# Gated unit on one core: second product's low part earlier in the ring, second half's weights on another queue, last rows' pieces respread

## The chip, the cores and the metric

The kernel runs on one core of one Trainium2 chip. The metric is the device time of one execution in microseconds (us); the median of the runs is what is compared. One execution was also profiled, and its trace gives the start and the length of each instruction on each engine: TensorE (PE, with its weight loads as PEld), VectorE (DVE), ScalarE (ACT), GpSimd (POOL), and SyncE (SP), which here only issues DMAs. Each engine works through its own instructions in order; semaphores make one wait for another.

## The reference

One block of a transformer in float32, for 2048 rows of 576 columns:

```
mod = (silu(c) @ w_mod) as six rows sa, ca, ga, sb, cb, gb of 576
h = layernorm(x) * (1 + ca) + sa
x = x + ga * (attention(h; 32 heads of 18, softmax over all 2048 keys) @ wo)
h = layernorm(x) * (1 + cb) + sb
x = x + gb * ((sigmoid(h @ w_gate) * (h @ w_up)) @ w_down)
```

The gated unit is the last line: w_gate and w_up are 576 x 4608, w_down is 4608 x 576.

## The kernel before, in words

Every product is formed from high and low parts: an operand is rounded to a shorter format for TensorE (the high part, F32R) and what the rounding dropped is a second operand (the low part). A product is high x high + high x low + low x high. "Low" stands below for making such a low part, a subtraction.

Attention comes first and takes the time up to about 1597 us of the trace. Near its end, the rows of its second half (rows 1024 to 2047) still lack the last 192 of 576 columns of the output projection; those columns go to DRAM (`oend`), the partial sums too (`x1p`), and the gated unit finishes these rows beside its own work.

**The gated unit** (from line 986 on) runs over two halves of the rows (1024 rows each), over 18 blocks of 256 of the 4608 columns, and over seven products in each block: gate and up together are formed in a scheme of seven products for a 2 x 2 split (in place of eight), so that some operands are sums of weight parts. `ORDER = (1, 6, 2, 7, 5, 4, 3)` is the order of the products. The loop at L1236 runs over `seq`, all 252 pairs of block and product; this document calls one pass a **turn**, numbers the turns of a block 0 to 6, and calls the turn number overall n. So turn 0 is product 1, turn 1 product 6 (the "second product"), turn 2 product 2, turn 3 product 7, turn 4 product 5, turn 5 product 4, turn 6 product 3.

In a turn TensorE does `product` (L1050): 14 matmuls, seven for the gate half and seven for the up half, which use the weight's high part (a = 0, 1, 2) and low part (a = 3, 4). The first low operand is the third matmul of each half. At turns 1 and 3 it also does `down` (L1090), the second matrix product of the block before: eight accumulators of six matmuls each, out of a pool of three PSUM banks, and VectorE adds each to the output (`Oa`, L1094). After a product VectorE adds up partial sums in PSUM (L1253 at turn 1, L1264 at turn 3, L1269 at turn 4, L1275 at turn 5, L1280 at turn 6). At turns 2, 4, 5 and 6 a quarter of the gated values is finished (`gate`): sigmoid on ScalarE (L1059, L1062), multiplication on VectorE (L1060, L1063), rounding on ScalarE (L1065), and the low part on VectorE (`gate_low`, L1070).

**The weights** come through a ring of five tiles (`wgp`, LOOK + 1 buffers). In the first half, three steps make the weights of a product:

- `weights_sums` (L998), on POOL: S1, S2, S3, the sums of raw weight parts that products 5, 6 and 7 use, made at turn 3 for the next block; at turn 1 S2 is rewritten for product 3, once product 6's low has read it. Emitted for turn n + 5, at the end of turn n.
- `weights_high` (L1018), on ScalarE (L1031): the rounding, for turn n + 4.
- `weights_low` (L1034), on VectorE: two subtractions, L1040 on 128 partitions and L1041 on 64, and then a DMA on SP (L1042) that stores the finished tile (640 KB) into `ws` in DRAM. `LOWS` says at which turn which low is made: an entry d at turn t makes that of turn t + d. The first one of a turn stands ahead of `gate_low`, the others behind it and behind a piece of the last rows.

In the second half, the same tiles are read back from `ws` (L1025), at the beginning of the turn four ahead, into the ring slot that the turn before has given up. Each block's w_down (`wd`, 1152 KB) is loaded by SP (L1074) at turn 4, into a single buffer that the down product of turn 3 has just given up.

**Order.** From turn n = 7 (`ORDERED`) the order on PE, DVE and ACT is that of the program text (`manual_schedule`); before it, and on POOL and SP throughout, the scheduler of the framework places instructions. A wait in one of these engines' instructions holds all that stands behind it there.

**The last rows** (`last_rows`, L1131) are a generator: each call of `next` does one piece, and its `yield` tells the loop what follows. Its pieces, in order: for two groups of four row tiles, a load of the columns (`od`), an empty one, a transposition with rounding into `oh` and `ol`, another with rounding into `om` (L1159 to L1161), and four projections (L1177, L1180); then for two groups, loads, an empty one, two statistics pieces (L159), a power on POOL, two Newton steps (L176 to L179), two normalisations, an empty one, and six transpositions that ScalarE modulates (L1185) and a DMA stores to `hs`; and last, three times, a load of tiles `B`, an empty one, and seven operand pieces: a subtraction on POOL (L740), a rounding on ScalarE (L729), a low part on POOL (L731, L736), and a store to `xs` on SP. The operands in `xs` are loaded for the second half in the last block of the first (L1305).

In the loop, a piece is done at turns 1 and 3 of each block, at every turn while `light` is true, and a second one at turn 1 unless the first yielded true:

```python
if n >= ROWS_FROM and (at in (1, 3) or light):
    light = next(rows2, None)
while lows:
    weights_low(n + lows.pop(0))
if n >= ROWS_FROM and at == 1 and not light:
    light = next(rows2, None)
```

The functions that the diff touches, and what calls them:

Of the kernel before, what the change touches and what calls it, by code (L numbers as in the profile page):

```python
# [15 lines left out]
F32 = mybir.dt.float32  # L16
# [25 lines left out]
DL = 384  # L42
ORDER = (1, 6, 2, 7, 5, 4, 3)
LOOK = 4
LOWS = ((1, 2), (2,), (2,), (2, 3, 4), (), (), ())
NB = F // 256
LAG = 2

# [2 lines left out]
SIDES = ((0, 0), (0, 1), (1, 0), (1, 1))  # L51
TURNED = ((0, 1), (0, 0), (1, 1), (1, 0)), ((0, 1), (1, 1), (0, 0), (1, 0))
ORDERED = 7
ROWS_FROM = 7
SECOND = 7 * NB


# [1 line left out]
def tile_block(ctx, tc, x_in, wqkv, wo, w_gate, w_up, w_down, c_in, w_mod, out):  # L59
    nc = tc.nc  # L60
# [105 lines left out]
    def ln_scales_steps(pool, mv, rs):  # L166

        n = rs.shape[-1]
        var = pool.tile([P, n], F32, name="var")
        sd = pool.tile([P, n], F32, name="sd")  # L170
        r0 = pool.tile([P, n], F32, name="r0")
        nc.vector.tensor_scalar_add(var, mv[:, :, 1], EPS)
        nc.gpsimd.tensor_tensor(r0, var, powers[:, 0:n], op=ALU.pow)
        yield True
        for to in (r0, rs):
            nc.vector.tensor_mul(sd, r0, r0)  # L176
            nc.vector.tensor_mul(sd, sd, var)
            nc.vector.tensor_scalar(sd, sd, -0.5, 1.5, op0=ALU.mult, op1=ALU.add)
            nc.vector.tensor_mul(to, r0, sd)  # L179
            yield to is r0  # L180

    def ln_apply(z, xt, mean, rs):

# [322 lines left out]
    with tc.tile_pool(name="wv1", bufs=1) as wvp:  # L506
        tiles = [[(o + D * w, P)] for o in (128, 256, 384) for w in (0, 1)] + [[(DM, 64), (D + DM, 64)]]
        for i, parts in enumerate(tiles):
# [5 lines left out]
            for g in range(2):  # L514
                pl = project_qk([(wt, 2 * g), (wt, 2 * g + 1)], run if i else None)
                col, n = parts[-1]
# [189 lines left out]
    def ln_spill(zs, ch, psum, pool, put):  # L706


        for g in range(2):
            for i in range(3):  # L710
                pt = psum()
                for j, z in enumerate(zs):
                    nc.tensor.transpose(pt[:, j * P : (j + 1) * P], z[:, g, i * P : (i + 1) * P], ident)
                ev = pool.tile([P, 512], F32, name="ev", bufs=2)
                c = 3 * g + i
                put(ev, pt, mcol2[:, 0, c : c + 1], mcol2[:, 1, c : c + 1])
                nc.sync.dma_start(hs[g, i, :, ch * 512 : (ch + 1) * 512], ev)
                yield c < 5

    def operand_parts(half, i, blocks, parts, hi, lo_eng, queue):  # L720

# [170 lines left out]
    for u in range(UNITS):  # L892
# [6 lines left out]
        for kt in range(NT):  # L899
# [6 lines left out]
            for does in (("vtmmttmvtm", "tmttkwmtmm") if plain else ("vmmttmmtvt", "mtkttmwmmt"))[kt % 2]:  # L906
# [16 lines left out]
                else:  # L923
                    c, h = next(sides)
# [93 lines left out]
    def weights_high(st, k):  # L1018

        w = wgp.tile([P, 2, 5, P], F32R, name="w")  # L1020
        st["w", k] = w
        kept = ws[st["b"], ORDER.index(k)]
        flat = w.rearrange("p v a c -> p (v a c)").bitcast(F32)
        if st["half"] == 1:
            nc.scalar.dma_start(flat, kept.bitcast(F32))  # L1025
            return
        A11, A12, A21, A22 = parts_of(st)
        src = {1: A11, 2: A12, 4: A22}.get(k)
        if src is None:
            src = st[{5: "S1", 6: "S2", 7: "S3", 3: "S2"}[k]]  # L1030
        nc.scalar.copy(w[:, :, 0:3, :], src)  # L1031
        st["src", k] = src
# [87 lines left out]
    for n in range(LOOK):  # L1120
        weights_sums(n)
        weights_high(block(n), seq[n][2])
    weights_low(0)
    weights_sums(LOOK)
    load(1, 0)
    load_x(4, "k2")
# [4 lines left out]
    def last_rows():  # L1131


        def psum():
            return pd.tile([P, 512], F32, name="d")

        with tc.tile_pool(name="fin", bufs=1, side="right") as pool:
            w = pool.tile([P, 2, 2, D], F32R, name="w")
            nc.gpsimd.dma_start(w, wod)
            for t0 in (0, 4):  # L1140
                od = pool.tile([P, 4, 256], F32, name="od")
                nc.sync.dma_start(od[:, :, 0:192], oend[:, t0 : t0 + 4, :])
                nc.sync.dma_start(od[:, :, 192:256], oend[:, t0 : t0 + 4, 128:192])
                yield True
                yield
                pt = psum()
                for j in range(4):
                    nc.tensor.transpose(pt[:, j * P : (j + 1) * P], od[:, j, 0:P], ident)
                oh = pool.tile([P, 512], F32R, name="oh")
                ol = pool.tile([P, 512], F32R, name="ol")  # L1150
                nc.vector.tensor_copy(oh, pt)
                nc.vector.tensor_sub(ol, pt, oh.bitcast(F32))
                yield
                pt = psum()
                for j in range(4):
                    nc.tensor.transpose(pt[:, j * P : (j + 1) * P], od[:, j, P:256], ident)
                om = pool.tile([P, 512], F32R, name="om")
                omh = pool.tile([P, 512], F32R, name="omh")
                nc.vector.tensor_copy(om[0:64], pt[0:64])  # L1159
                nc.vector.tensor_copy(omh[64:P], pt[64:P])  # L1160
                nc.vector.tensor_sub(om[64:P], pt[64:P], omh[64:P].bitcast(F32))  # L1161
                xts = []
                for j in range(-1, 4):
                    if j < 3:
                        xts.append(pool.tile([P, D], F32, name="xt", bufs=2))
                        nc.sync.dma_start(xts[-1], x1p[:, t0 + j + 1, :])
                    if j < 0:
                        yield
                        continue
                    rows = slice(j * P, (j + 1) * P)  # L1170
                    xt = xts[j]
                    for h in range(2):
                        cols = slice(h * HALF, (h + 1) * HALF)
                        acc = psum()
                        ts_ = ((oh, 0, 0), (oh, 1, 0), (ol, 0, 0), (om, 0, 1), (om, 1, 1))
                        for n, (a, i, k) in enumerate(ts_):
                            nc.tensor.matmul(  # L1177
                                acc[:, :HALF], a[:, rows], w[:, i, k, cols], start=n == 0, stop=n == 4
                            )
                        nc.vector.tensor_add(xt[:, cols], xt[:, cols], acc[:, :HALF])  # L1180
                    nc.sync.dma_start(x1d[:, t0 + j, :], xt)
                    yield

        def modulated(ev, pt, scale, bias):
            nc.scalar.activation(ev, pt, AF.Identity, scale=scale, bias=bias)  # L1185

        with tc.tile_pool(name="zp2", bufs=1, side="right") as zp:
            for ch in (2, 3):
                zs = []
                for t in range(4 * ch, 4 * ch + 4):  # L1190
                    z = zp.tile([P, 2, 384], F32, name="z", bufs=4)
                    for g in range(2):
                        nc.sync.dma_start(z[:, g, 0:HALF], x1d[:, t - 8, g * HALF : (g + 1) * HALF])
                    zs.append(z)
                yield True
                yield
                for j, z in enumerate(zs):
                    ln_stats(zp, z[:, :, 0:HALF], mv2[:, 4 * ch + j, :])
                    if j % 2:
                        yield  # L1200
                four = slice(4 * ch, 4 * ch + 4)
                yield from ln_scales_steps(zp, mv2[:, four, :], rs2[:, four])
                for j, z in enumerate(zs):
                    ln_rows(z, 4 * ch + j, z[:, :, 0:HALF], nc.vector)
                    if j % 2:
                        yield j > 1
                yield True
                yield from ln_spill(zs, ch, psum, zp, modulated)
        with tc.tile_pool(name="xop2", bufs=2) as pool:

            def get():
                return [pool.tile([P, 512], F32, name="B", bufs=5) for _ in range(5)]

            def parts():
                return pool.tile([P, 2, 512], F32R, name="ho", bufs=3)

            for i in range(3):
                blocks = get()
                for (g, r), t in zip(((0, 0), (0, 1), (1, 0), (1, 1)), blocks):
                    cols = slice(HW + r * 512, HW + (r + 1) * 512)  # L1220
                    nc.sync.dma_start(t, hs[g, i, :, cols])
                yield True
                yield True
                for _ in operand_parts(1, i, blocks, parts, nc.scalar.copy, nc.gpsimd, nc.sync):
                    yield True
# [5 lines left out]
        return t[:, 512 * v : 512 * (v + 1)]  # L1231

    rows2 = last_rows()
    light = False
    before = None
    for n, (hf, b, k) in enumerate(seq):  # L1236
        if n == ORDERED:
            manual.enter_context(tc.manual_schedule(engines={mybir.EngineType.PE, mybir.EngineType.DVE, mybir.EngineType.Activation}))
        st, kept = block(n), None
# [14 lines left out]
        elif k == 2:  # L1254
# [4 lines left out]
            kept = gate(st, None, 0, 0)  # L1259
# [5 lines left out]
        elif k == 5:  # L1265
# [4 lines left out]
            kept = gate(st, st["u3"], 1, 1)  # L1270
            down_weights(st)
        elif k == 4:
# [3 lines left out]
            kept = gate(st, st["p1"], 1, 0)  # L1276
        else:
# [3 lines left out]
            kept = gate(st, st["u2"], 0, 1)  # L1281
# [4 lines left out]
        at = n % 7  # L1286
        lows = list(LOWS[at])
        if lows:
# [3 lines left out]
        if n >= ROWS_FROM and (at in (1, 3) or light):  # L1292
            light = next(rows2, None)
        while lows:
            weights_low(n + lows.pop(0))
        if n >= ROWS_FROM and at == 1 and not light:
            light = next(rows2, None)
        weights_sums(n + LOOK + 1)
        if at in (0, 4):
# [36 lines left out]
```

## Time and profile before

| what | value |
|---|---|
| median of three runs | 2979.63 us (2979.29 to 2982.65) |
| the profiled execution's own time | 2975.26 us |
| its span, first to last instruction | 2973.5 us |
| PE busy | 2863.7 us, 96% of the span |
| DVE busy | 2208.8 us, 74% |
| ACT busy | 1564.3 us, 53% |
| POOL busy | 709.2 us, 24% |
| mean granted TensorE clock | 0.987 |
| `ws` stores on SP, loads of `w` on ACT | 126 and 126, 640 KB each |

The profile lists, for each group of instructions, the line of the kernel, the engine, the operation, "output <- input" by the program's names, the shapes, and how many. In a timeline, a row gives the start, the length, the instruction, and in brackets how long the engine had been idle before it and who released it. A list of waits gives, for each pair, the total, the number of times, and the longest. A stretch ("windows") gives the busy time of each engine between two points, the granted clock (1.00 is full), the share of the DMA engines' time, and GB/s. The chain is the work that ended last, followed back from the end. Because matmuls are pipelined, a row of many matmuls is a little longer than the distance to the next.

### The profile page before, as it was taken

How to read it: one execution, taken by the hardware profiler on the slowest of the kernel's cores; microseconds unless marked ns; L12 is line 12 of the kernel's file. 1: busy time of each engine (PE TensorE's matmuls, PEld its weight loads, DVE VectorE, ACT ScalarE, POOL GpSimd, SP SyncE). 2: the span in 40 equal slices, each digit the busy share in tenths (PEclk: the TensorE clock that was granted, in tenths of full speed). 3: DMA queues.
4: the chain of work that ended last, by engine and by line, in shares of the span. 5: the costliest groups of instructions: out<-in, count | busy, mean ns of one | idle time of the engine just before them, and what ended most of it. 6: DMA issues, size and time to landing. Idle time of an engine off the chain costs nothing.

```text
span 2973.5 us, 46334 instructions
## 1 busy us (share of the span) xinstructions
PE 2863.7 (96%) x17141; PEld 1892.2 (64%) x17141; DVE 2208.8 (74%) x4015; ACT 1564.3 (53%) x2941; POOL 709.2 (24%) x869
## 2 busy tenths in 40 slices
PE   7999999999999999999999999899989999999998
PEld 6964333333344444444445888788877888888887
DVE  7277888888899989999874777778777555555555
ACT  3216889999987779988786222233333111111111
POOL 3122024445122112750112222222463100000000
PEclk9999999999999999999999999999999999999999
DMA  5344124333212111321236556565776844555443
GB/s 170 122 160 124 57 69 139 138 130 123 75 57 63 47 38 50 107 84 47 79 108 232 192 192 219 183 233 191 271 243 238 313 157 171 166 170 173 159 157 125
DMA packets 136386, 429.26 MB, mean 144 GB/s; under 512 B 19100, under 2 KB 55968, under 8 KB 123872
## 3 DMA queue, kind: packets, MB, share of 16 engines
q1 hardware_dynamic: 101520, 261.62, 25.9%
q10 hardware_dynamic: 18144, 82.58, 8.4%
q0 software_dynamic: 16496, 82.10, 7.9%
q8 instruction: 135, 2.21, 0.3%
q14 instruction: 91, 0.75, 0.1%
HBM read 267.77 MB, written 157.95 MB: 143 GB/s over the span
## 4 chain that ended last, share of the span: by engine, by line
PE 80%; DVE 9%; ACT 5%; DMA 2%; issue 2%; POOL 1%; SPq 1%; ACTq 0%; DVEq 0%; POOLq 0%
PE x L1050 18%; PE o L551 16%; PE d L1090 15%; PE s L449 11%; PE s L927 10%; PE s L277 3%; ACT p L931 3%; PE s L688 2%; PE s L328 2%; DVE w L1040 1%; DVE w L1041 1%; DVE mx L455 1%; DMA ws<-w 1%; DVE hl L1070 1%; ACT hh L1065 1%
## 5 line engine op out<-in xcount | busy, mean ns | idle before, releaser
L455 DVE TENSOR_REDUCE mx<-s 128x1 f32<-128x512 f32 x1696 | 1076.1, 683 | 122.5 <-PE s L449 107.7
L931 ACT ACTIVATE p<-s 128x512 f32<-128x512 f32 x2048 | 1068.7, 610 | 147.8 <-PE s L449 78.0
L449 PE MATMUL s<-k,q 54*128 54x512 f32 x1920 | 607.7, 450 | 13.0 <-ACT p L931 5.9
L551 PE MATMUL o<-p,vaug 128*32 128x512 f32 x4096 | 554.1, 606 | 0.4 <-ACT p L931 0.4
L927 PE MATMUL s<-q,k 56*128 56x512 f32 x1920 | 551.7, 425 | 0.7 <-DMA q<-mrows 0.2
L1090 PE MATMUL d<-wd,hh 128*128 128x288 f32 x2304 | 462.8, 295 | 11.9 <-DVE Oa L1094 11.9
L927 PEld LDWEIGHTS s<-q,k 56*128 56x128 f32 x1920 | 260.2, 186 | 293.4 <-DVE mx L455 183.8
L449 PEld LDWEIGHTS s<-k,q 54*128 54x128 f32 x1920 | 273.2, 184 | 250.4 <-ACT p L931 170.4
L1050 PE MATMUL x<-k,w 128*128 128x512 f32 x1512 | 379.1, 405 | 43.4 <-DVE w L1040 40.5
L1094 DVE TENSOR_TENSOR Oa<-Oa,d 128x288 f32<-128x288 f32 x576 | 260.2, 454 | 173.5 <-PE d L1090 169.6
L1090 PEld LDWEIGHTS d<-wd,hh 128*128 128x128 f32 x2304 | 375.4, 189 | 19.6 <-DVE Oa L1094 13.6
L1050 PEld LDWEIGHTS x<-k,w 128*128 128x128 f32 x1512 | 292.7, 196 | 110.8 <-DVE w L1040 47.3
L1090 PE MATMUL d<-wd,hl 128*128 128x288 f32 x1152 | 341.0, 296 | 0.0
L1062 ACT ACTIVATE u<-u 128x512 f32<-128x512 f32 x72 | 45.5, 632 | 421.6 <-DVE u L1269 381.1
L1050 PE MATMUL x<-big,w 128*128 128x512 f32 x1008 | 236.8, 390 | 2.6 <-DVE u L1269 2.6
L1050 PE MATMUL x<-w,w 128*128 128x512 f32 x1008 | 235.8, 391 | 0.0
L1090 PEld LDWEIGHTS d<-wd,hl 128*128 128x128 f32 x1152 | 217.0, 188 | 0.0
L1050 PEld LDWEIGHTS x<-big,w 128*128 128x128 f32 x1008 | 188.3, 188 | 44.0 <-issue 4.4
L1050 PEld LDWEIGHTS x<-w,w 128*128 128x128 f32 x1008 | 187.9, 188 | 37.3
L1059 ACT ACTIVATE sg<-x 128x512 f32<-128x512 f32 x36 | 21.5, 599 | 346.9 <-PE x L1050 346.7
L551 PEld LDWEIGHTS o<-p,vaug 128*32 128x32 f32 x4096 | 83.4, 108 | 164.0 <-issue 152.3
L1096 POOL DMA_DIRECT2D out_dram<-Oa x16 | 8.7, 544 | 620.8 <-DVE Oa L1094 620.7
(215 smaller groups left out, 3002.4 us busy)
## 6 DMA issues: line engine op xcount, KB each, us to landing
ws<-w SPq DMA_DIRECT2D x126, 640.0 KB
w<-ws ACTq DMA_DIRECT2D x126, 640.0 KB
wd<-wds SPq DMA_DIRECT2D x36, 1152.0 KB
k<-kd SPq DMA_DIRECT2D x60, 360.0 KB
wds<-w POOLq DMA_DIRECT2D x18, 1152.0 KB, 4.5
k<-kd SPq DMA_DIRECT2D x60, 180.0 KB
w<-in_B_w_down_dram POOLq DMA_DIRECT2D x18, 576.0 KB, 4.6
q<-qd SPq DMA_DIRECT2D x64, 144.0 KB
```

Source lines behind the costliest of these rows:

```text
L277: nc.tensor.matmul(acc, w, hT[:, t, cols], start=n == 0, stop=n == len(ts_) - 1)
L328: nc.tensor.matmul(acc[:, 0:HALF], hT[:, k, rows], w, start=n == 0, stop=n == len(ts_) - 1,)
L449: nc.tensor.matmul(sp, qs[rows, qt * P : (qt + 1) * P], ks[rows, at * 512 : (at + 1) * 512], start=True, stop=True,)
L455: nc.vector.tensor_reduce(to, sp, axis=AX.X, op=ALU.max)
L551: nc.tensor.matmul(acc[32 * j : 32 * j + 32, :], vaug[:, kt, (2 * p + h) * VW : (2 * p + h) * VW + 32], probs[2 * c + h], start=kt == 0, s ...
L688: nc.tensor.matmul(acc[:, :HALF], a, w, start=i == 0, stop=i == len(ts_) - 1)
L927: nc.tensor.matmul(sT, ks[rows, kcols], qs[rows, c * 512 : (c + 1) * 512], start=True, stop=True)
L931: state["exp"] = nc.scalar.activation(pr, sT, AF.Exp, scale=SCALE)
L1050: nc.tensor.matmul(acc[v], w[:, v, a, :], X[s][:, b, :], start=first and n == 0, stop=n == 6, skip_group_check=not first,)
L1062: nc.scalar.activation(t[:, 0:512], t[:, 0:512], AF.Sigmoid)
L1090: nc.tensor.matmul(acc[:, :HALF], a[:, f, rows], w[:, f, cols], start=n == 0, stop=n == 5)
L1094: nc.vector.tensor_add(Oa[:, t, cols], Oa[:, t, cols], acc[:, :HALF])
```

## The change

- `LOWS`: the low of product 6 leaves turn 0, where it was made one turn ahead of its use, for turn 5 of the block before, three turns ahead (`(3,)` at index 5). There it stands ahead of that turn's `gate_low`. Since block 0 has no block before it, the loop is preceded by the lows of turns 0 and 1 in place of turn 0 alone.
- The second half's reads of `ws` (L1025) are issued by SP in place of ACT.
- The last rows start at n = 4 in place of 7, and `light` now has three values: True (a further piece at once, and at turns 1 and 3 a second one behind it), None (a second one at turn 1 alone), and 0 (neither). The piece that makes `om` yields 0, so that no projection follows in its turn. An empty piece behind a load now falls into the same turn as the load; of the operand pieces and of the modulated transpositions, two are done at turn 3.

Worked out from the two loops, in n (block:turn): the first rounding `oh`, `ol` moves from 10 (1:3) to 8 (1:1), the first `om` from 15 (2:1, with a projection in the same turn) to 8 (1:1), the first projection from 15 to 10 (1:3); the second `oh`, `ol` from 29 (4:1) to 24 (3:3). Statistics, Newton steps and normalisations keep their turns. Operand pieces were at 87 to 111, with a load and an empty piece between the three groups, seven of them in block 15; they are now at 86 to 105, one of them in block 15.

```diff
-LOWS = ((1, 2), (2,), (2,), (2, 3, 4), (), (), ())
+LOWS = ((2,), (2,), (2,), (2, 3, 4), (), (3,), ())
...
-ROWS_FROM = 7
+ROWS_FROM = 4
...
             nc.vector.tensor_mul(to, r0, sd)
-            yield to is r0
+            yield True if to is r0 else None
...
                 nc.sync.dma_start(hs[g, i, :, ch * 512 : (ch + 1) * 512], ev)
-                yield c < 5
+                yield True if c < 5 else None
...
         if st["half"] == 1:
-            nc.scalar.dma_start(flat, kept.bitcast(F32))
+            nc.sync.dma_start(flat, kept.bitcast(F32))
             return
...
-    weights_low(0)
+    for n in range(2):
+        weights_low(n)
...
                     if j < 0:
-                        yield
+                        yield 0
                         continue
...
                     if j % 2:
-                        yield j > 1
+                        yield True if j > 1 else None
...
     rows2 = last_rows()
-    light = False
+    light = True
...
-        if n >= ROWS_FROM and at == 1 and not light:
+        if n >= ROWS_FROM and (at == 1 and light is None or at in (1, 3) and light is True):
             light = next(rows2, None)
```

## The prediction

> **What bounds the kernel now.** I read the page first, then the stretches of the gated unit, then what TensorE waits for in each. A turn is one of the seven products of a block, turns 0 to 6 in ring order; "low" is the pair of VectorE subtractions L1040 and L1041.
>
> ```profile
> span 2973.5 us, 46334 instructions
> PE 2863.7 (96%) x17141; PEld 1892.2 (64%) x17141; DVE 2208.8 (74%) x4015; ACT 1564.3 (53%) x2941; POOL 709.2 (24%) x869
> ```
>
> ```profile
> 1598.00:2347.00 749.00, 690.67 (x3692) 602.61 (x3693) 549.78 (x947) 221.57 (x342) 236.53 (x207) 0.96 0.65 232
> 2347.00:2973.00 626.00, 617.03 (x3438) 549.61 (x3436) 342.79 (x607) 106.60 (x176) 7.61 (x14) 1.00 0.49 164
> ```
>
> TensorE is busy 96% of the span, so only what it waits for can be won. The two stretches are the gated unit's first half (18 blocks, and 4 turns of the next) and the rest of the second; columns are length, busy PE, PEld, DVE, ACT, POOL, granted clock, DMA share and GB/s. The second is full: 617 of 626 us, clock 1.00. The first has 58 us of idle PE and a clock of 0.96. TensorE's waits from 1599 to 2347 us (total, times, longest), then those of the second half:
>
> ```profile
> PE x L1050 <- DVE w L1040: 40.5, 14, 4.3
> PE d L1090 <- DVE Oa L1094: 10.5, 6, 6.0
> PE d L1177 <- DVE om L1161: 2.9, 1, 2.9
> PE x L1050 <- DVE u L1269: 2.6, 5, 1.0
> ...
> PE x L1050 <- DVE w L1041: 0.4, 1, 0.4
> ```
>
> ```profile
> PE d L1090 <- DVE Oa L1094: 1.4, 1, 1.4
> ```
>
> The first row is the target: nearly once a block TensorE waits for a low. Block 4 shows which, first on PE, then on DVE:
>
> ```profile
> 1740.03 3.35 PE L1050 MATMUL x<-k,w 128*128 128x512 f32 x14
> 1743.21 6.51 PE L1050 MATMUL x<-big,w 128*128 128x512 f32 x28
> 1749.56 3.79 PE L1050 MATMUL x<-k,w 128*128 128x512 f32 x16
> 1755.72 3.01 PE L1050 MATMUL x<-k,w 128*128 128x512 f32 x12 [2.38 <-DVE w L1040]
> ```
>
> ```profile
> 1744.81 1.29 DVE L1269 TENSOR_TENSOR u<-x,u 128x512 f32<-128x512 f32 x2
> ...
> 1748.24 1.28 DVE L1275 TENSOR_TENSOR p<-x,p 128x512 f32<-128x512 f32 x2
> ...
> 1751.01 0.69 DVE L1070 TENSOR_TENSOR hl<-p,hh 128x512 fp32r<-128x512 f32 x1 [0.69 <-ACT hh L1065]
> 1751.62 1.28 DVE L1280 TENSOR_TENSOR u<-x,u 128x512 f32<-128x512 f32 x2
> ...
> 1754.38 0.69 DVE L1070 TENSOR_TENSOR hl<-u,hh 128x512 fp32r<-128x512 f32 x1 [0.68 <-ACT hh L1065]
> 1754.99 0.68 DVE L1040 TENSOR_TENSOR w<-S,w 128x512 fp32r<-128x512 f32 x1
> 1755.70 0.42 DVE L1041 TENSOR_TENSOR w<-S,w 64x256 fp32r<-64x256 f32 x1
> 1756.16 0.69 DVE L1040 TENSOR_TENSOR w<-raw,w 128x512 fp32r<-128x512 f32 x1
> 1756.88 1.13 DVE L1041 TENSOR_TENSOR w<-raw,w 64x256 fp32r<-64x256 f32 x1
> 1758.04 1.50 DVE L1253 TENSOR_TENSOR u<-x,p 128x512 f32<-128x512 f32 x2
> 1759.56 0.46 DVE L1094 TENSOR_TENSOR Oa<-Oa,d 128x288 f32<-128x288 f32 x1
> 1760.36 0.45 DVE L1094 TENSOR_TENSOR Oa<-Oa,d 128x288 f32<-128x288 f32 x1 [0.34 <-PE d L1090]
> ```
>
> Turns 4, 5, 6 and 0 have no down product; each costs TensorE 3.18 us (two issue in 6.35, 1743.21 to 1749.56). VectorE needs 3.4 us for each of turns 4 to 6 (1748.24 to 1751.62): two adds, the multiplication, 0.69 idle for ScalarE's rounding, the low part of h. It starts late, and only then comes the low of product 6. TensorE does product 1 and two matmuls of product 6 (x16), then stops.
>
> **Part 1, the low of product 6 at turn 5.** It now stands in front of L1070 in turn 5, into the 0.69 us hole ahead of 1751.01; its 0.68 + 0.42 us are done near 1751.5, 1.8 us before x16 ends. So the wait goes: 40.5 + 0.4 = **40.9 us**. What ScalarE must round first is there: the low already follows turn 4's rounding, in its old place too. The low's store goes along on SP, among the loads of the next block's weights; its slot in the ring is not wanted again before turn 2, so this costs nothing, and were it late, ScalarE's rounding would wait there. With the wait goes a slower clock behind it; the first and the last of the 15 resumptions, by the chain (block 4's above took 3.01):
>
> ```profile
> 1668.61 4.57 PE x L1050 x12
> ...
> 2280.99 4.47 PE x L1050 x12
> ```
>
> Six of the 15 take 3.0; the excess of the other nine over that, 1.4 to 2.8 each, adds up to **15.8 us**.
>
> [...] The gap of 3.02 us before 1668.61 was followed by a slow stretch, so here I go by the rows.
>
> **What is late next.** The 1.12 us do not vanish; they fill the hole and push turn 6 by 0.4. Then the second low of turn 0 and L1253 follow, and L1253 stands ahead of the down products' sums in VectorE's order. Without the wait, block 4's down product would start at 1755.91 (1749.56 + 6.35); with three accumulators of 0.8 us each (the spacing of the L1094), the fourth waits for the first L1094 at 1758.3. VectorE then ends L1253 at 1759.54 - 1.17 + 0.43 = 1758.8, L1094 at 1759.3: a wait of **up to 1.0** us. POOL's rewriting of S2 moves with the low: it slowed turn 0's second L1041 (1.13 against 0.42), giving 0.7 back there, and now falls beside turns 5 and 6. Ends 0.2 and 1.0; I take 0.6 for each of the 11 blocks that are not in the operand pieces: **+6.6**.
>
> Some blocks carry a piece of the last rows at turn 3, in front of the lows. Rows: a statistics piece, one operation of a Newton piece, and what statistics did at turn 6:
>
> ```profile
> L159 DVE BATCH_NORM_STATS2 st<-z x16: 406/442/461, 1861.6 to 2011.2; 128x6 f32<-128x288 f32 x16
> ```
>
> ```profile
> 1904.88 0.16 DVE L179 TENSOR_TENSOR rs<-r,sd 128x4 f32<-128x4 f32 x1
> ```
>
> ```profile
> 1867.37 3.44 PE L1050 MATMUL x<-big,w 128*128 128x512 f32 x14 [0.96 <-DVE u L1269]
> ```
>
> Four of the former are 1.8 us, 0.96 of which TensorE waits already; with the two aggregations 1.0 more will show, twice. The Newton piece has four of the latter: 0.65, twice. The rounding of the attention's columns (two operations on a 128x512 tile, each like L1040's 0.69) is now at block 3, with the transposes on TensorE as some relief: 1.0. **+4.3**.
>
> **Part 3, the pieces spread.** They start at turn 4 of block 0 and no longer idle two turns at a time. At block 2 the rounding into `om` and a projection shared a turn: 2.9 us and, as behind most such gaps, some 1.6 of slow clock. Now that rounding is done at block 1, ahead of the projection at turn 3; I keep 0.5 for VectorE's longer queue there: **-4.0**. The loads of `od` and `wod` go out at turn 4 of block 0, four turns ahead of their use (two before); I cost them at nothing, and late they would cost at most about such a gap again. The low of block 0's product 6, now ahead of the loop, is hidden behind product 1. The 21 operand pieces move from turns 87-111 to 86-105, seven in each of blocks 12 to 14, two of them at turn 3. What they cost VectorE, by a plain block and one with such pieces:
>
> ```profile
> 1725.00:1764.00 39.00, 36.53 (x203) 32.08 (x203) 28.68 (x50) 11.11 (x17) 9.64 (x8) 1.00 0.61 219
> 2129.00:2170.00 41.00, 36.95 (x196) 32.02 (x196) 30.41 (x49) 13.88 (x22) 21.06 (x17) 0.96 0.74 261
> ```
>
> ```profile
> L731 POOL TENSOR_TENSOR ho<-B,ho x14: 1268/1295/1439, 2097.5 to 2192.9; 128x512 fp32r<-128x512 f32 x14
> L1040 DVE TENSOR_TENSOR w<-raw,w x54: 682/692/1820, 1597.1 to 2305.0; 128x512 fp32r<-128x512 f32 x54
> ```
>
> 11.4 us more of POOL went with 1.7 more of VectorE. Seven pieces at about 2.6 us are 18 us of POOL, 2.8 of VectorE; with a share of the plain block's 0.6, I take 3 us in each of three blocks (bounds 0.6 and 6) and two stretches of slow clock at 1.6: **+12.2**. Their DMA also crowds: 0.74 of the engines at 41 us a block.
>
> [...]
>
> **Part 2, the second half's weights on SP.** In steady state nothing waits there (1.4 us, at the end), so 0. At the change of halves something does: a stored weight lands late, ScalarE is held at its DMA issue, its copy of product 1 comes late, and VectorE behind it.
>
> ```profile
> 2307.32 18.39 DMA ws<-w
> ```
>
> ```profile
> 2326.51 0.59 ACT L1247 COPY p<-x 128x512 f32<-128x512 f32 x1 [3.17 <-DMA ws<-w]
> ```
>
> ```profile
> 2328.83 0.85 PE L1090 MATMUL d<-wd,hh 128*128 128x288 f32 x2 [6.04 <-DVE Oa L1094]
> ```
>
> On SP this wait holds only the loads behind it. 6.0 and, at the least that was seen above, 1.4 of slow clock go; product 2's weights now queue behind that store and may be 1 us late: **-6.4** (ends 0 and -7.4). Queued behind an SP wait are later weights and `wd`, used three turns on or more.
>
> **Sum.** -56.7 + 6.6 + 4.3 - 4.0 + 12.2 - 6.4 = -44.0. The profiled run took 2975.26 (span 2973.5 and 1.8 around it): 2931.3. The median of the timed runs lies 4.4 above it, so I forecast **2936**.
>
> **Rivals.**
> - *All of it comes back*: VectorE's slack suffices everywhere and the operand pieces cost nothing. Only 4.3 of the returns stay: -62.8, **2917**. For: VectorE is busy 549.78 of 749. Against: block 4's slack above is negative. 0.17.
> - *The wait changes its name*: 2 us a block on L1094 or L1269, and 6 plus 1.6 in the operand blocks: 22 + 4.3 + 22.8 returned, -18, **2962**. For: six such waits exist (10.5 us). 0.16.
> - *Nothing is moved*: POOL's sums or ScalarE's rounding reach turn 5 as late as turn 0, the low waits there, and all behind it: **2980**. Against, from block 5, where the low would now stand at about 1788.9: 0.05.
>
> ```profile
> 1782.31 2.59 POOL L1009 TENSOR_TENSOR S<-S,raw 128x384 f32<-128x384 f32 x2 [7.84 <-DVE w L1041]
> ```
>
> ```profile
> 1786.75 0.84 ACT L1031 CAST w<-S 128x768 fp32r<-128x768 f32 x1
> ```
>
> - *Slower: SP's queue in the second half.* One queue carries seven weights and `wd` a block. A weight is issued four turns ahead, at the tightest 4 x 3.18 = 12.7 us. Above that landing time each block loses the rest; at the 18.39 us that a store took, 5.7 x 18 = 102: **3038**. Against: DMA share 0.49. 0.07.
>
> **Chances.** The forecast (2922 to 2950) has 0.55. This kernel can be told from no change by about 0.2%, 6 us. Faster 0.55 + 0.17 + 0.16 = 0.88, same 0.05, slower 0.07. 2912 to 2964 holds the forecast and most of the first two rivals, 0.8.
>
> **What would show it.** Right: no row "PE x L1050 <- DVE w L1040" of more than a few us; small waits on L1094 in its place, largest in blocks 12 to 14; clock near 0.99 before 2347; no gap at the change of halves; the second half at 626 us. Wrong: waits on L1094 or L1269 of over 2 us in plain blocks; waits for ws in those blocks; PE idle in the second half.

## The result, and the profile after

| | before | after |
|---|---|---|
| median | 2979.46 us (2978.76 to 2982.65) | 2937.47 us (2933.89 to 2941.94) |
| ratio | | 0.9858, interval 0.9841 to 0.9875 |
| the profiled execution's own time | 2975.26 us | 2941.94 us |
| gated unit in that trace, first L1050 to the end | 2973.5 - 1599.1 = 1374.4 us | 2940.2 - 1602.2 = 1338.0 us |

The forecast was 2936 (2912 to 2964). In the changed kernel the lines behind L1123 stand one lower: L1269 is now L1270, L1253 is L1254, L1161 is L1162, L1185 is L1186. First the two stretches, cut at the same points of the work as before (columns as there):

```profile
1601.00:2314.00 713.00, 677.19 (x3694) 595.81 (x3695) 547.25 (x948) 221.82 (x342) 234.38 (x207) 0.99 0.68 243
2314.00:2940.00 626.00, 616.70 (x3436) 549.44 (x3434) 342.57 (x607) 106.63 (x176) 8.49 (x16) 1.00 0.49 165
```

The second stretch takes the same 626 us. The first went from 749 to 713. Idle TensorE fell from 749 - 690.67 = 58.3 to 713 - 677.19 = 35.8 us, that is by 22.5; the same matmuls were busy for 13.5 us less, at a clock of 0.99 in place of 0.96. What TensorE still waits for in the first stretch (total, times, longest):

```profile
PE d L1090 <- DVE Oa L1094: 18.1, 15, 4.0
PE x L1050 <- DVE u L1270: 10.6, 6, 3.3
PE d L1090 <- ACT ev L1186: 4.7, 2, 2.8
PE x L1050 <- ACT w L1031: 2.4, 1, 2.4
PE x L1050 <- DMA w<-ws: 1.1, 1, 1.1
```

The row of 40.5 us on L1040 is gone, and `om` too (2.9). The 2.4 stand at the unit's start, in both kernels. VectorE from turn 5 of block 4 to turn 1 of block 5, a stretch without costly pieces, shows how:

```profile
1778.37 0.69 DVE L1040 TENSOR_TENSOR w<-S,w 128x512 fp32r<-128x512 f32 x1
1779.09 0.42 DVE L1041 TENSOR_TENSOR w<-S,w 64x256 fp32r<-64x256 f32 x1
1779.54 0.69 DVE L1070 TENSOR_TENSOR hl<-p,hh 128x512 fp32r<-128x512 f32 x1
...
1783.32 0.69 DVE L1070 TENSOR_TENSOR hl<-u,hh 128x512 fp32r<-128x512 f32 x1 [0.69 <-ACT hh L1065]
1783.93 0.69 DVE L1040 TENSOR_TENSOR w<-raw,w 128x512 fp32r<-128x512 f32 x1
1784.64 0.42 DVE L1041 TENSOR_TENSOR w<-raw,w 64x256 fp32r<-64x256 f32 x1
1785.10 1.29 DVE L1254 TENSOR_TENSOR u<-x,p 128x512 f32<-128x512 f32 x2
1786.30 1.35 DVE L1094 TENSOR_TENSOR Oa<-Oa,d 128x288 f32<-128x288 f32 x3
```

The low of block 5's product 6 (1778.37) stands where VectorE idled 0.69 us for ScalarE in turn 5; L1070 behind it starts without a wait. Behind turn 6 one low is left, it takes 0.42 in its L1041 and not 1.13, and L1254 ends at 1786.4; TensorE doesn't wait in that turn.

### The profile page after: what moved, and what is told of

It is laid out like the page before. It is cut to its first block, busy times and chain, and to the rows that moved or that the text cites. A ratio compares the mean times of both kernels' runs of the same rounds, so it can differ in the third digit from the quotient of the medians.

```text
span 2940.2 us, 46375 instructions
## 1 busy us (share of the span) xinstructions
PE 2851.2 (97%) x17141; PEld 1884.8 (64%) x17141; DVE 2205.7 (75%) x4015; ACT 1564.5 (53%) x2941; POOL 707.2 (24%) x869
## 5 line engine op out<-in xcount | busy, mean ns | idle before, releaser
L1090 PE MATMUL d<-wd,hh 128*128 128x288 f32 x2304 | 467.7, 298 | 24.2 <-DVE Oa L1094 19.5
L1090 PEld LDWEIGHTS d<-wd,hh 128*128 128x128 f32 x2304 | 377.5, 190 | 34.1 <-DVE Oa L1094 23.4
L1094 DVE TENSOR_TENSOR Oa<-Oa,d 128x288 f32<-128x288 f32 x576 | 257.7, 453 | 173.7 <-PE d L1090 169.7
L1050 PE MATMUL x<-k,w 128*128 128x512 f32 x1512 | 357.9, 391 | 2.4 <-ACT w L1031 2.4
L1090 PE MATMUL d<-wd,hl 128*128 128x288 f32 x1152 | 342.6, 297 | 0.0
L1050 PEld LDWEIGHTS x<-k,w 128*128 128x128 f32 x1512 | 282.6, 189 | 59.8 <-ACT w L1031 2.6
L1050 PE MATMUL x<-big,w 128*128 128x512 f32 x1008 | 238.8, 392 | 10.6 <-DVE u L1270 10.6
L1050 PE MATMUL x<-w,w 128*128 128x512 f32 x1008 | 235.2, 390 | 1.1 <-DMA w<-ws 1.1
L1050 PEld LDWEIGHTS x<-big,w 128*128 128x128 f32 x1008 | 189.2, 189 | 53.0 <-issue 12.5
L1090 PEld LDWEIGHTS d<-wd,hl 128*128 128x128 f32 x1152 | 218.7, 190 | 0.0
L1050 PEld LDWEIGHTS x<-w,w 128*128 128x128 f32 x1008 | 187.3, 188 | 38.5 <-issue 1.3
```

The source lines that it names most:

```text
L1050: nc.tensor.matmul(acc[v], w[:, v, a, :], X[s][:, b, :], start=first and n == 0, stop=n == 6, skip_group_check=not first,)
L1090: nc.tensor.matmul(acc[:, :HALF], a[:, f, rows], w[:, f, cols], start=n == 0, stop=n == 5)
L1094: nc.vector.tensor_add(Oa[:, t, cols], Oa[:, t, cols], acc[:, :HALF])
```

## What took the time that is left

The largest waits stand from 2070 to 2225 us, where the operand pieces are. The waits of that stretch, then turn 4 of block 14 on PE, on DVE, and on POOL:

```profile
PE d L1090 <- DVE Oa L1094: 9.2, 3, 4.0
PE x L1050 <- DVE u L1270: 7.9, 3, 3.3
```

```profile
2169.30 4.87 PE L1050 MATMUL x<-big,w 128*128 128x512 f32 x14 [3.26 <-DVE u L1270]
```

```profile
2160.09 0.68 DVE L1040 TENSOR_TENSOR w<-raw,w 128x512 fp32r<-128x512 f32 x1
2160.81 1.39 DVE L1041 TENSOR_TENSOR w<-raw,w 64x256 fp32r<-64x256 f32 x1
2162.23 1.67 DVE L1040 TENSOR_TENSOR w<-S,w 128x512 fp32r<-128x512 f32 x1
2163.92 1.42 DVE L1041 TENSOR_TENSOR w<-S,w 64x256 fp32r<-64x256 f32 x1
2165.36 1.66 DVE L1040 TENSOR_TENSOR w<-raw,w 128x512 fp32r<-128x512 f32 x1
2167.06 1.37 DVE L1041 TENSOR_TENSOR w<-raw,w 64x256 fp32r<-64x256 f32 x1
2168.46 1.29 DVE L1270 TENSOR_TENSOR u<-x,u 128x512 f32<-128x512 f32 x2
```

```profile
2160.10 4.95 POOL L736 TENSOR_TENSOR ho<-B,ho 32x512 fp32r<-32x512 f32 x3
2165.13 1.35 POOL L740 TENSOR_TENSOR B<-B 128x512 f32<-128x512 f32 x1
2166.55 1.59 POOL L736 TENSOR_TENSOR ho<-B,ho 32x512 fp32r<-32x512 f32 x1
```

Turn 3 makes three lows. Five of the six subtractions take 0.95 to 1.00 us longer than the 0.68 and 0.42 they take elsewhere, together 4.9 us, and POOL is subtracting all that time. In block 4, which has no operand pieces, five of the six take 0.68 and 0.42; the last L1041 takes 1.12 there too, beside POOL's own sums of weights (L1009). So 4.2 us of the 4.9 come with the operand pieces, and of these TensorE, which awaits L1270, sees 3.26.

The second new wait is on ScalarE. In a list of instructions, its output tile `ev` for the modulated transpositions:

```profile
2057.08 0.78 ACT L1186 ACTIVATE ev<-d,mcol 128x512 f32<-128x512 f32 x1 [1.60 <-DMA hs<-ev]
```

```profile
2057.91 0.54 PE L1090 MATMUL d<-wd,hh 128*128 128x288 f32 x2 [2.84 <-ACT ev L1186]
```

ScalarE waits for a buffer of `ev` whose store to DRAM is not yet through; the PSUM bank that it should empty is one of the three of the down product, so TensorE waits as well. Two of these pieces now share turn 3, but that isn't the whole cause: where each has a turn to itself, 2.6 us (e1), 2.9 (e4) and 2.1 (e11) of this wait are there as well, and a second profile of the changed kernel (e12) has 3.0 in place of 4.7.

## The experiments

"Gated unit" below is, as in the table, the length from the first L1050 to the end of the profiled execution; it leaves out the attention, whose end lay between 1599 and 1605 us from kernel to kernel though none changes it. Kernels e1 to e4 were timed on one chip, e5 to e9 on another, e10 to e12 on a third, each group beside runs of before on that chip.

### Each part alone

**e1_low_only**: before with:

```diff
-LOWS = ((1, 2), (2,), (2,), (2, 3, 4), (), (), ())
+LOWS = ((2,), (2,), (2,), (2, 3, 4), (), (3,), ())
-    weights_low(0)
+    for n in range(2):
+        weights_low(n)
```

> The kernel before with only the low of product 6 moved to turn 5 (and the second low ahead of the loop). Theory A (the low carried most of the gain): the 40.9 us of waits on L1040 and about 16 us of slow clock go; about 5 us come back as waits on L1094 and L1269 in blocks with statistics, Newton and rounding pieces, about 15 us in the four blocks with operand pieces (single ones, as before); the wait at the rounding into om and the gap at the change of halves stay. About 36 us below the kernel before, 2943 us. Rival B (the wait only changes its name): at most 12 us below, 2968 or more.

Measured: 2945.33 us against 2978.76, ratio 0.9887 (0.9874 to 0.9901). The low row is gone; its waits for VectorE in the first half:

```profile
PE d L1090 <- DVE Oa L1094: 26.6, 17, 5.6
PE x L1050 <- DVE u L1270: 3.2, 5, 1.0
PE d L1178 <- DVE om L1162: 2.9, 1, 2.9
```

33.4 of the 42 us come with this part alone, as theory A had it. The wait at the change of halves (5.6) and that on `om` (2.9) stay, as they must.

**e2_sp_only**: before with:

```diff
-            nc.scalar.dma_start(flat, kept.bitcast(F32))
+            nc.sync.dma_start(flat, kept.bitcast(F32))
```

> The kernel before with only the second half's weight loads on SP. Theory A: the 6.0 us gap at the change of halves and some 1.4 us of slow clock go, about 1 us comes back as a wait for a load: 6 us below the kernel before, 2973 us; the rest of the second half unchanged at 626 us for its 626. Rival B (the gap is made by the DMA engines' load, not by who issues): the gap stays in another place, 0 to 2 us.

Measured: 2973.55, ratio 0.998 (0.9971 to 0.9989), 5.2 us less. In its waits the 6.04 us on L1094 at the change of halves are gone, and a wait on a stored weight stands there:

```profile
PE d L1090 <- DVE Oa L1094: 4.4, 5, 1.3
...
PE x L1050 <- DMA w<-ws: 1.0, 1, 1.0
```

e3_spread_only: after without the two edits above, that is, the last rows alone respread.

> The kernel before with only the pieces of the last rows respread. Theory A (spreading gains at the rounding and loses at the doubled pieces): minus 4.5 us at block 2 and minus 7 at block 16, which has no operand pieces any more; plus 4.7 from the doubled transpositions at blocks 9 and 12, plus 4 to 12 in blocks 12 to 14: between 2976 and 2986 us. Rival B (the spread is a gain by itself): 10 us or more below, under 2969.

Measured: 2985.17, ratio 1.0019 (1.0009 to 1.0029): by itself the spread costs 6.4 us. The wait on `om` is gone from its list, but these two rows grew (40.5 and 2.6 before):

```profile
PE x L1050 <- DVE w L1040: 44.5, 16, 5.1
...
PE x L1050 <- DVE u L1269: 7.4, 5, 3.3
```

The three add up to -32.2 us, and all at once give -42.0. Where the 10 us lie was tried by pairs, with the changed kernel again beside them.

e11_low_and_sp: e1_low_only with e2's line.

> The kernel before with the low of product 6 at turn 5 and the second half's loads on SP; the last rows' pieces as before. Alone, the low took 33.4 us off, the queue 5.2, and the spread added 6.4: together -32.2, where the changed kernel is 42.0 faster. Theory A: the missing 10 us lie between the low and the spread: the spread costs 6 only while the low stands at turn 0, and gives 3 to 4 once it stands at turn 5. Then this kernel is 2979 - 33 - 5 = 2940 to 2941. Theory B: they lie between the low and the queue. Then this kernel is about 2930, and the spread costs 6 here too.

e10_low_and_spread: after with L1025 back on `nc.scalar`.

> The changed kernel with the second half's loads back on ScalarE's queue. Theory A (the missing 10 us lie between low and spread): the queue is worth its own 5 here, 2942 to 2943, with the wait of about 6 at the change of halves back. Theory B (they lie between low and queue): without the queue only the low's 33 and the spread's +6 are left, about 2952.

e12_after_again: after, unaltered.

> The changed kernel unaltered, for a comparison on the same chip: 2937 (2934 to 2942).

Measured, against 2981.13 on that chip: 2940.47 (0.9871, 0.985 to 0.9892), 2946.71 (0.9891, 0.9874 to 0.9908), and 2939.21 (0.9861, 0.9839 to 0.9883). Theory A holds for the larger part: with the low moved, the spread neither costs nor gives what can be measured (2939.21 against 2940.47; 34.4 us below before with the spread, 33.4 without). The 6.4 us that it costs alone belong to the low at turn 0. The queue is worth 7.5 us here (2946.71 - 2939.21) in place of 5.2, so some 2 us of the 10 stand there, near the scatter. For the same reason e10 came out between what its two theories gave (2942 to 2943, and 2952). In e11 the waits at the operand pieces are there as well, spread over more blocks and under another name; of this row, which is for the whole first half, 12.3 us stand from 2070 to 2300 us:

```profile
PE d L1090 <- DVE Oa L1094: 21.0, 16, 4.0
```

### Why the operand pieces cost so much

Two causes were in question: that two pieces now share turn 3, or that POOL's subtractions lengthen VectorE's, however the pieces are shared out.

**e4_single_pieces**: after with:

```diff
-                yield True if c < 5 else None
+                yield 2 if c < 5 else None
...
                 for _ in operand_parts(1, i, blocks, parts, nc.scalar.copy, nc.gpsimd, nc.sync):
-                    yield True
+                    yield 2
```

> The changed kernel, but operand pieces and modulated transpositions one a turn, not two at turn 3. Theory A (two pieces at turn 3 are what still costs there): the 4.7 us of TensorE waits on the transpositions' ScalarE work go, and of some 26 us of waits and slow clock in blocks 12 to 15 about a third: 8 to 12 us below the changed kernel. Rival B (the amount of GpSimd work in a block matters, not how it lies): the 4.7 go, the operand blocks stay as they are: 3 to 5 us below.

Measured: 2936.6, ratio 0.9859 (0.9846 to 0.9873); after has 2937.47. The gain that theory A expected isn't there, so it fell; B, with 3 to 5 us, is nearer, but neither was right in full: of the 4.7 us on `ev`, which both had go, 2.9 stayed. With one piece a turn, the operand pieces reach further, to turn 3 of block 15, and each block pays on L1094. Its waits from 2070 to 2225 us:

```profile
PE d L1090 <- DVE Oa L1094: 14.5, 5, 4.0
PE x L1050 <- DVE u L1281: 1.1, 3, 0.4
```

So POOL itself was taken away.

**e5_no_pool_operands**: after with, in the second half's operands:

```diff
+                if half == 1:
+                    for v in (i, i + 3):
+                        queue.dma_start(xs[half, s, :, v, :].bitcast(F32), ho[:, 0, :].bitcast(F32))
+                    return
...
+                    if half == 0:
                         lo_eng.tensor_sub(lo, t[q : q + 32], lo.bitcast(F32))
...
+            if half == 0:
                 nc.gpsimd.tensor_tensor(to, a, b, op=ALU.subtract)
+        if half == 1:
+            t3 = b22
```

> The changed kernel with GpSimd's part of the second half's operand pieces left out: no subtractions for the sums of the operands and no low parts (the high part is stored twice, so the same bytes move; the output's second half of the rows is not the reference's). ScalarE's roundings and the DMAs stay. Theory A (GpSimd's reads beside VectorE make the waits of blocks 12 to 15): of the 17 us of waits there and 8.5 us of slow clock at most 5 us stay, 20 us below the changed kernel, 2917 us; L1040 and L1041 take 0.69 and 0.42 there. Rival B (ScalarE held by roundings that wait for stores, or crowded DMA): the waits stay above 10 us and the time within 8 us of the changed kernel.

Measured: 2919.41, ratio 0.9801 (0.9785 to 0.9818); 18 us below after, 20 below e12. From 2070 to 2225 us one row is left:

```profile
PE d L1098 <- DVE Oa L1102: 1.2, 4, 0.5
```

That is what was expected without POOL's part. Rounding, stores and VectorE's own list are still there, so nearly the whole operand cost is POOL's. The wait on `ev` (5.2) is still there too, so the 18 to 20 don't hold it. Is it that POOL is busy, or what it does? e6 keeps POOL's instructions in their places, but they read nothing:

**e6_pool_memset**: after with, for the second half, twice each:

```diff
-                    lo_eng.tensor_sub(lo, t[q : q + 32], lo.bitcast(F32))
+                        nc.gpsimd.memset(lo.bitcast(F32), 0.0)
...
-            nc.gpsimd.tensor_tensor(to, a, b, op=ALU.subtract)
+                    nc.gpsimd.memset(to, 0.0)
```

> The changed kernel with the same GpSimd instructions replaced by two memsets each to the same tiles (the operand sums and low parts are left out, so the output's second half of the rows is not the reference's): GpSimd writes at the same places and holds the same order, but reads nothing. Theory A1 (what slows VectorE is GpSimd's reading of SBUF): as without GpSimd's work, 2917 to 2922 us, VectorE's rows at their usual length. Rival A2 (any GpSimd instruction beside VectorE slows it): the waits in blocks 12 to 15 stay at half or more of 17 us, and L1040 beside a memset takes over 1 us.

Measured: 2919.74, ratio 0.98 (0.9781 to 0.982), as without POOL; from 2070 to 2225 us 3.7 us of waits are left in place of 17.1. Its DVE and POOL at turn 3 of block 14 (L1052 and L1053 are the low here):

```profile
2149.41 0.68 DVE L1052 TENSOR_TENSOR w<-raw,w 128x512 fp32r<-128x512 f32 x1
2150.13 0.42 DVE L1053 TENSOR_TENSOR w<-raw,w 64x256 fp32r<-64x256 f32 x1
2150.58 0.69 DVE L1052 TENSOR_TENSOR w<-S,w 128x512 fp32r<-128x512 f32 x1
```

```profile
2148.51 2.24 POOL L742 MEMSET ho<- 32x512 f32 x4 [0.81 <-POOL B L750]
2150.81 0.53 POOL L750 MEMSET B<- 128x512 f32 x1
2151.40 0.52 POOL L742 MEMSET ho<- 32x512 f32 x1
```

POOL is as closely packed as in the changed kernel, and the lows take 0.68 and 0.42. So a POOL that was merely busy didn't lengthen them; one that subtracted, and so read two operands from SBUF, did (1.37 to 1.67 in block 14). The memsets are shorter than the subtractions (0.53 against some 1.3 us), so length wasn't held equal; that one long instruction which reads nothing would do no harm isn't shown.

The rows of block 14 give the size: five of VectorE's six subtractions lose 0.95 to 1.00 us each, beside subtractions of POOL that take 1.35 to 1.65. The additions of L1254, L1265 and L1270, which have one input in PSUM, lose nothing: none of their 216 in the changed kernel takes over 0.70 us, L1270's two beside a POOL subtraction at 2168.46 included. Nor do the memsets cost time: 2919.74 with them, 2919.41 without POOL's part. How POOL's subtractions hold up VectorE's isn't shown by these runs.

### The wait on `ev`, and a better place

**e7_three_ev**: after with:

```diff
-                ev = pool.tile([P, 512], F32, name="ev", bufs=2)
+                ev = pool.tile([P, 512], F32, name="ev", bufs=3)
```

> The changed kernel with three buffers in place of two for the modulated transpositions (ev). Theory A (ScalarE waits for a store of the buffer two before it, keeps an accumulator bank, and TensorE waits for that bank): the 4.7 us of TensorE waits on L1186 go, 4 to 5 us below the changed kernel, 2933 us. Rival B (ScalarE is late for other reasons): the waits on L1186 stay, same time.

Measured: 2934.88, ratio 0.9852 (0.9835 to 0.9869), 2.6 us below after; at four runs each, and on another chip, that lies within the scatter. The wait itself is gone: no row of the first half names `ev`, and those on L1094 (14.8) and L1270 (11.8) stay. So theory A's cause is shown, though not its 4 to 5 us.

The last kernel leaves POOL its work, but moves the operand pieces to turns 0 to 2, away from turn 3's three lows, over blocks 12 to 16:

**e9_pieces_in_slack**: e7_three_ev with:

```diff
-                yield True
-                yield True
-                for _ in operand_parts(1, i, blocks, parts, nc.scalar.copy, nc.gpsimd, nc.sync):
-                    yield True
+                yield 6
+                for q, _ in enumerate(operand_parts(1, i, blocks, parts, nc.scalar.copy, nc.gpsimd, nc.sync)):
+                    yield 3 if q < 6 else 5
...
-        if n >= ROWS_FROM and (at in (1, 3) or light):
+        if n >= ROWS_FROM and (at in (0, 1, 2) if light in (3, 6) else at in (1, 3) or light):
...
-        if n >= ROWS_FROM and (at == 1 and light is None or at in (1, 3) and light is True):
+        if n >= ROWS_FROM and (at == 1 and light is None or at in (1, 3) and light is True or at in (1, 2) and light == 3 or light == 5):
```

> The changed kernel with three ev buffers and the operand pieces only at turns 0 to 2 (one, two, two), with their loads at once behind the piece before; they run from block 12 turn 2 to block 16 turn 2. Theory A (it matters whether GpSimd works beside the chain of turns 3 to 0, where VectorE has no slack): of the 26 us of waits and slow clock in blocks 12 to 15 at most 8 stay, and the 4.7 go: 20 to 25 us below the changed kernel, 2912 to 2917 us. Rival B (the amount of GpSimd work counts wherever it lies): 5 us from ev alone, 2932 us or more.

Measured: 2918.88 (2915.67 to 2921.9), ratio 0.9799 (0.9782 to 0.9817): 18.6 us below after and 61.4 below before, the fastest kernel here that does all the work. It is 2 us above the range that was expected (2912 to 2917), and 16.0 below e7, which was timed on the same chip and differs by the places of the operand pieces alone. From 2070 to 2225 us its waits are

```profile
PE d L1090 <- DVE Oa L1094: 4.4, 5, 1.2
PE x L1050 <- DVE u L1269: 2.5, 1, 2.5
```

That is 6.9 us in place of 17.1. The 2.5 us stand in block 15, the one in which POOL, after a wait of 2.77 us for a load of `B`, still subtracts beside most of turn 3's lows; on DVE and on PE:

```profile
2182.00 1.67 DVE L1040 TENSOR_TENSOR w<-S,w 128x512 fp32r<-128x512 f32 x1
```

```profile
2187.83 3.46 PE L1050 MATMUL x<-big,w 128*128 128x512 f32 x14 [2.48 <-DVE u L1269]
```

The place does matter, then, once the pieces leave the turn with three lows, where e4 had still left some: what POOL's work costs depends on what VectorE does beside it. That a block now holds fewer pieces doesn't account for it: from 2188 to 2224 us, the lows of turn 3 in block 15 to those in block 16, POOL does 14.6 us of such work and TensorE waits 2.0; in the changed kernel, the same stretch from block 12 to 13 (2076 to 2117 us) has 15.5 us of it and 5.6 of waits.

## Why the prediction was right, point by point

The total and its main cause were right; two terms were mis-sized in opposite directions, and one wait was missed. In the profiled pair (us; waits of TensorE from the lists, clock from its busy time; the +4.0 is what the lists leave: 34.5 after, without 17.1, 4.7, 1.1 and 0.5, less 10.5 + 2.6 - 6.0 = 7.1 before; the 2.4 at the unit's start, in both, are left out):

| step of the prediction | predicted | measured |
|---|---|---|
| part 1: waits for the low of product 6 | -40.9 | -40.9, the rows are gone |
| returned in plain blocks | +6.6 | +0.5 |
| statistics, Newton and rounding pieces, with all else | +4.3 | +4.0 |
| part 3: wait on `om` | -2.4 | -2.9 |
| operand pieces, waits | +9.0 | +17.1 |
| wait on `ev` | none | +4.7 |
| part 2: change of halves, wait | -5.0 | -5.0 (6.04 to 1.1) |
| sum of the waits | -28.4 | -22.5 |
| slow clock, all parts | -15.6 | -13.5 |

- **Part 1 was right in mechanism and size.** The hole in turn 5 took the low (block 5), and e1 alone gave 33.4 us.
- **Plain blocks: too dear by 6.** 0.6 us in each of 11 blocks was the middle between 0.2 and 1.0. Blocks 2, 3, 5 and 6 have no such wait; the last blocks of the half have these two, on PE:

```profile
2225.11 0.54 PE L1090 MATMUL d<-wd,hh 128*128 128x288 f32 x2 [0.24 <-DVE Oa L1094]
...
2260.58 0.53 PE L1090 MATMUL d<-wd,hh 128*128 128x288 f32 x2 [0.23 <-DVE Oa L1094]
```

The upper end took L1041's 1.13 and L1253's 1.50 us of before as given. L1041 fell to 0.42, since POOL's rewriting of S2 moved away from it with the low: 0.7 us that the prediction had named and only half counted. L1253's pair fell to 1.29 for another reason: each of its additions took at most 0.69 us in before too, and the 1.50 held a wait for TensorE, which was late itself.
- **Statistics, Newton and rounding pieces: right, term by term.** New waits on L1094 stand at turn 1 of blocks 7 and 10 (0.85 each, behind statistics; predicted 1.0), 8 and 11 (0.89 and 0.82, behind Newton steps; 0.65) and 4 (0.86, behind the rounding; 1.0). One normalisation of each group also moved by a turn, to turn 3 (from 53 to 52 and from 74 to 73), unlike what the section on the change says; it shows in no wait, as e11, which keeps the old turns, has 0.87 and 0.88 in blocks 8 and 11.
- **Operand pieces: too cheap by half.** The 3 us a block came from VectorE's mean in one block of before, where the pieces were thinner. The mean hid what decides: turn 3 has three lows in a row and TensorE waits right behind them, so of the 4.2 us that the pieces cost VectorE there 3.3 show at once, and the L1094 of turn 1 are late once more in each block (2.6 to 4.0). With the slow clock it was 18 to 20 us by e5, against 12.2 predicted. The turns were a little off as well: worked out from the loop, blocks 12 to 15 have 6, 7, 7 and 1 of the 21 pieces, not seven in each of three. A subtraction beside POOL's lost 0.95 to 1.00 us, but only where POOL was subtracting, and it cost time only where TensorE waited for it.
- **Part 3: the wait on `om` went; the buffers of `ev` were not looked at.** The prediction followed VectorE's queue for the doubled pieces at turn 3 and not ScalarE's output tiles. Some 2 to 3 us of that wait come even without doubled pieces (e1, e4, e11), once the low is moved. And the spread as a whole was worth nothing that can be measured (e11 beside e12).
- **Part 2 was right**, 5.2 us alone against 6.4, with the wait of 1 us for product 2's weight that it forecast (1.1). SP's queue cost nothing that shows: the second half took 626 us again, so the rival on the slower side fell.
- **The rival "all of it comes back"** gave 2917, which e5 (2919.4) and e9 (2918.9) come near to once the operand pieces are out of the way: VectorE's slack does suffice in plain blocks.
- **The last step, from the profiled execution to the median, held partly by chance.** The sum of -44.0 stands against -36.4 for the gated unit of the profiled pair: 7.6 us too good. The attention in the profile after ended 3.1 us later, so that the two executions differ by 33.3 only, and the forecast of the profiled one, 2931.3, was 10.6 us too low. The prediction then put the median 4.4 above it, as in before; it came 4.5 below, which gives back 8.9 of the 10.6. The medians differ by 42.0, and the second profile of the changed kernel (e12) has 2936.5 - 1602.2 = 1334.3 us for its gated unit, 40.1 below before. Why one execution differs by 4 us from the next isn't shown.

## What to carry to other kernels

A wait in an in-order queue goes away when its cause is moved into a hole that the engine idles through anyway; look for the hole by its releaser (0.69 us for ScalarE's rounding) and count what must still fit behind it. When work is spread over turns, ask not how much an engine has to do per block, but which turn ends in something that is awaited: moving the same 21 pieces into turns 0 to 2, away from the turn with three lows, took 16 us off (e7 and e9). Parts of a change do not add up when they share a queue: the spread cost 6 us with the old order and nothing with the new.

## What the runs showed of the hardware

**VectorE beside GpSimd.** In block 14, five of six subtractions of two SBUF operands took 0.95 to 1.00 us longer beside POOL's subtractions; beside POOL's memsets (e6) they took no longer than usual (0.68 and 0.42), and none of the 216 additions of L1254, L1265 and L1270, which have one input in PSUM, took over 0.70 us.

**The clock after short gaps.** In the changed kernel's PE, a gap of 2.95 us was followed by full speed (14 matmuls in 3.44 us, granted clock 1.00), and one of 2.62 us by a stretch in which pairs of L1090 take 0.68 in place of 0.43 (granted clock 0.61 from 2100.69 to 2105 us):

```profile
2085.00 3.44 PE L1050 MATMUL x<-big,w 128*128 128x512 f32 x14 [2.95 <-DVE u L1270]
...
2099.78 0.53 PE L1090 MATMUL d<-wd,hh 128*128 128x288 f32 x2 [2.62 <-DVE Oa L1094]
...
2100.28 0.43 PE L1090 MATMUL d<-wd,hh 128*128 128x288 f32 x2
...
2100.69 0.68 PE L1090 MATMUL d<-wd,hh 128*128 128x288 f32 x2
```

The kernel before shows the same, on rows of twelve matmuls behind a wait for a low: 3.16 us of gap without a loss (granted clock 1.00 in that row), 2.39 with one (0.64).

```profile
2200.51 3.04 PE L1050 MATMUL x<-k,w 128*128 128x512 f32 x12 [3.16 <-DVE w L1040]
...
2280.99 4.47 PE L1050 MATMUL x<-k,w 128*128 128x512 f32 x12 [2.39 <-DVE w L1040]
```

Of the 14 waits on L1040 in the list of before, nine were followed by a slow stretch (gaps of 1.80 to 4.27 us) and five were not (1.79 to 3.16 us). What decides between two gaps of this length isn't shown by these runs. For the whole change, the prediction's sum by rows was 15.6 us less of slow clock; 13.5 were measured.
